# Reordering the loads of an attention and expert kernel: the first v in halves, q and k two steps ahead, the conversions of v early in a step

## The chip, the cores and the metric

The kernel runs on one core of a Trainium2 chip. The metric is device time in microseconds (us) of one launch; lower is better. A core has a matrix engine (TensorE, PE in the profile; its weight loads are PEld), three engines that work on rows of memory (VectorE or DVE, ScalarE or ACT, GpSimd or POOL), and a queue engine (SyncE, SP). Each engine works through its own list of instructions in order and waits where it needs another's result. Transfers between main memory and the core's on-chip memory (DMA) are issued here by POOL (the profile's queue q0, which can convert float32 to 16 bits on the way) and by SP (queue q1, which copies). Both queues share the same 16 DMA engines.

## What is computed

Sliding-window attention over 8 batches, 8 heads, 576 positions and 64 columns, then, for each batch, one expert of eight, chosen from the mean over the positions:

```python
mask = (rel >= 0) & (rel < 64)                       # attention, per batch and head
attn = softmax(where(mask, q @ k.T / 8, -1e9))
x    = attn @ v                                      # to [batch, 576, 512]
...
logits = x.mean(axis=1) @ w_gate                     # the gate, per batch
e      = argmax(logits);  g = softmax(logits)[e]
out    = g * (relu(x @ w1[e]) @ w2[e])               # 512 -> 1024 -> 512
```

The weights of an expert can be fetched only when the gate of its batch is known.

## The kernel before

The work of attention is cut into 16 units: unit u is one half of a batch (four heads), so batch b has the units 2b and 2b+1. A unit goes through these functions:

- `load_qk(u)` (line 208) issues two DMAs from POOL, q and k of the unit, 288 KB each on the chip, into six rotating buffers.
- `load_v(b)` (line 217) loads v of a whole batch as float32. The DMA is issued by SP, but a one-column memset on POOL in the same buffer stands ahead of it, so that it starts only when POOL has come to that place in its own list. There are two buffers.
- `transpose_qk` (line 324) turns q or k on PE; `leave_qk` (line 337) copies q out on ACT, and k on DVE unless told otherwise.
- `scores(u, c)` (line 361), c = 0 to 2: the products on PE, the exponential on ACT (line 384), the mask on DVE (line 386).
- `cast_part(u, part)` (line 300) makes the 16-bit copies of v that the products with v need: "whole" converts the unit's half of v into `va`, "low" and "high" copy it, shifted, into `vb`; `cast_v(u)` does all three. All stand on DVE unless told otherwise. The first of them is what waits for the DMA of v.
- `values(u, s)` (line 393), s = 0 and 1: the products with v on PE (line 408), then the division by the row sums on DVE (lines 422 and 424). It needs all three masked score blocks and the copies of v.
- `transpose_x(u)` (line 436) turns the result on PE, and copies it out with sums on ACT, from which DVE builds the input of the gate.

When both units of batch b are done, `gate(b)` (line 482) runs one small matmul (line 484), a maximum and its place on DVE (lines 488 and 490), and POOL loads the number of the expert into a register. Then `load_w1(b)` and `load_w2(b)` fetch 1 MB each (on the chip) through POOL. `expert_up` (line 543) is eight chunks with w1, `expert_down` (line 563) five with w2, whose results DVE copies and SP sends out.

Everything stands in an order written out by hand: `P(...)` keeps program order. Ahead of the loop the first four units are written out one call after another; `busy(n)` issues n matmuls on nothing, which keep PE at work. Then comes a loop over steps t = 4 to 19. Step t holds the scores and values of unit t, the transposes and conversions of unit t+1, and a share of the chunks of the experts, given out by `experts(pace)`. On even steps the gate of batch t/2 − 1 follows, with its loads.

In this version q and k are loaded up to four units ahead: before the loop as far as unit 6, at t = 4 unit 7 behind w2, at t = 5 the units 8 and 9, then unit t+4. The conversions of unit t+1 are spread over the second half of step t: "whole" after the transpose of q, "low" after `values(t, 0)`, "high" after `values(t, 1)`. w1 of batch 0 comes in four quarters, and `expert_up(0, ft)` uses quarter ft // 2.

## Time and profile before

| | |
|---|---|
| three runs, median (lowest to highest) | 235.81 us (235.61 to 236.13) |
| the profiled execution's own time | 237.41 us |
| its span, first to last instruction | 235.7 us |
| mean granted TensorE clock | 0.973 |
| busy: PE, PEld, DVE, ACT, POOL | 207.7, 141.4, 142.3, 121.5, 42.8 us |
| read from main memory, written | 61.90 MB, 9.44 MB |

The timeline of an engine gives start, duration, engine, line, operation, output<-input, shape and count; in brackets stands the engine's idle time ahead of it and what ended that. The chain of waits goes back from the last instruction and names at each step what had to end; its rows are start, duration, what. The DMA view of a stretch of time gives the packets and bytes of each queue, and for each kind of transfer issued there the time from issue to landing. The table of stretches gives the busy time of each engine within each stretch, with the granted TensorE clock.

### The profile page before, as it was taken

Reading aid. Unit: us, or ns where it says so; the run is one execution under the profiler, and the core shown is the slowest. Engines: PE = TensorE matmul, PEld = TensorE weight load, DVE = VectorE, ACT = ScalarE, POOL = GpSimd, SP = SyncE. Lnnn points to the kernel's source line nnn. Section 1 sums busy time; section 2 is a strip of 40 time slices with the busy share of each in tenths; the row PEclk is TensorE's granted clock in tenths of the full one; section 3 lists DMA queues with packets and bytes.
Section 4 is the critical chain, followed back from the end, with each engine's and each line's share of the span. In section 5 each row is a group of like instructions: output and inputs, shape, how many; then the busy total and the mean of one; then the engine's idle time right before and its main releaser. Section 6 shows DMA issues by size and latency. Waiting matters only on the chain.

```text
span 235.7 us, 7000 instructions
## 1 busy us (share of the span) xinstructions
PE 207.7 (88%) x3020; PEld 141.4 (60%) x3020; DVE 142.3 (60%) x315; ACT 121.5 (52%) x205; POOL 42.8 (18%) x72
## 2 busy tenths in 40 slices
PE   7657879979799978999899989999999999998980
PEld 2427557725478545875578556865687558647640
DVE  2559597539856594838764697559675964531140
ACT  2461576933376606693467617680758265605500
POOL 7252192041300160007000330020001100200000
PEclk9995899979999999999999999999999999999997
DMA  5999299999999999997999999999960995199342
GB/s 76 221 216 256 47 116 220 236 243 246 228 247 265 246 243 250 230 247 152 228 244 235 198 180 261 229 253 173 246 177 3 161 233 169 11 197 237 116 145 66
DMA packets 31222, 45.64 MB, mean 194 GB/s; under 512 B 2512, under 2 KB 22992, under 8 KB 31184
## 3 DMA queue, kind: packets, MB, share of 16 engines
q0 software_dynamic: 15152, 26.22, 63.2%
q1 hardware_dynamic: 15232, 18.88, 26.7%
q8 instruction: 25, 0.41, 0.7%
q10 hardware_dynamic: 800, 0.03, 0.2%
q14 instruction: 13, 0.11, 0.1%
HBM read 61.90 MB, written 9.44 MB: 303 GB/s over the span
## 4 chain that ended last, share of the span: by engine, by line
PE 46%; DMA 24%; ACT 11%; DVE 11%; issue 3%; POOL 1%; POOLq 1%; SPq 0%
PE php L555 23%; DMA w1t<-in_moe_w_dram 19%; PE pso L569 9%; DMA vn<-in_v_dram 5%; PE tp L329 5%; PE op L408 4%; ACT xT L453 4%; ACT pt L384 4%; ACT hT L559 3%; DVE vb L298 2%; DVE dst L298 2%; DVE pt L386 2%; PE tp L445 2%; DVE ob L572 1%; PE sp L369 1%
## 5 line engine op out<-in xcount | busy, mean ns | idle before, releaser
L555 PE MATMUL php<-xT,w1t 128*128 128x288 f16 x512 | 71.5, 288 | 5.3 <-DMA w1t<-in_moe_w_dram 4.7
L559 ACT ACTIVATE hT<-php,gatew 128x576 f16<-128x576 f32 x64 | 47.4, 746 | 33.3 <-PE php L555 33.3
L569 PE MATMUL pso<-w2t,hT 128*128 128x512 f16 x256 | 61.6, 386 | 2.6 <-DMA w2t<-in_moe_w_dram 1.8
L555 PEld LDWEIGHTS <-w1t 128*128 128x128 f16 x512 | 53.6, 113 | 13.3 <-DMA w1t<-in_moe_w_dram 5.6
L384 ACT ACTIVATE pt<-sp 128x768 f16<-128x768 f32 x48 | 37.7, 813 | 13.8 <-PE sp L369 13.8
L569 PEld LDWEIGHTS <-hT 128*128 128x128 f16 x256 | 23.4, 99 | 29.2 <-issue 3.0
L453 ACT ACTIVATE xT<-tp 128x576 f16<-128x576 f16 x28 | 17.9, 646 | 33.5 <-PE tp L445 33.5
L572 DVE COPY ob<-pso 128x512 f32<-128x512 f32 x32 | 21.9, 685 | 19.9 <-PE pso L569 19.6
L386 DVE TENSOR_TENSOR pt<-pt,masks 128x768 f16<-128x768 f16 x42 | 23.1, 557 | 17.3 <-ACT pt L384 16.8
L531 POOL DMA_DIRECT2D w1t<-in_moe_w_dram x7 | 5.0, 717 | 139.0 <-DVE gatew L513 75.1
L424 DVE TENSOR_TENSOR x<-op,linv 128x640 f16<-128x640 f32 x32 | 26.4, 824 | 1.1
L342 ACT COPY dst<-tp 128x1152 bf16<-128x1152 bf16 x16 | 18.0, 1124 | 12.1 <-PE tp L329 12.1
L298 DVE COPY dst<-tp 128x1152 bf16<-128x1152 bf16 x15 | 20.3, 1350 | 4.3 <-PE tp L329 4.0
L408 PE MATMUL op<-vb,pt 128*64 128x65 f16 x320 | 17.7, 202 | 4.1 <-DVE vb L298 3.5
L408 PEld LDWEIGHTS <-pt 128*64 128x64 f16 x640 | 14.4, 116 | 10.7 <-issue 6.0
L408 PE MATMUL op<-va,pt 128*64 128x65 f16 x320 | 17.4, 202 | 0.0
L369 PE MATMUL sp<-dst 64*64 64x128 bf16 (+1 forms) x672 | 15.4, 214 | 1.9 <-DVE dst L298 1.9
L298 DVE CAST va<-vn 128x1152 f16<-128x1152 f32 x16 | 12.7, 796 | 5.9 <-DMA vn<-in_v_dram 5.8
L298 DVE COPY vb<-va 64x1152 f16<-64x1152 f16 (+1 forms) x30 | 15.8, 527 | 0.6
L369 PEld LDWEIGHTS <-dst 64*64 64x64 bf16 x672 | 10.4, 106 | 8.9 <-issue 4.4
L476 DVE SCALAR_TENSOR_TENSOR gpart<-wg,pooled,gpart 128x8 f32<-128x8 f32 x21 | 4.8, 226 | 17.9 <-ACT xT L453 17.9
L445 PE MATMUL tp<-identh,x 128*128 128x128 f16 x160 | 11.6, 220 | 3.3 <-DVE x L424 2.5
(69 smaller groups left out, 166.6 us busy)
## 6 DMA issues: line engine op xcount, KB each, us to landing
w2t<-in_moe_w_dram POOLq DMA_DIRECT2D x8, 1024.0 KB, 17.5
out_dram<-ob SPq DMA_DIRECT2D x32, 256.0 KB, 8.6
w1t<-in_moe_w_dram POOLq DMA_DIRECT2D x7, 1024.0 KB, 10.2
qn<-in_q_dram POOLq DMA_DIRECT2D x16, 288.0 KB, 15.3
kn<-in_k_dram POOLq DMA_DIRECT2D x16, 288.0 KB, 16.5
w1t<-in_moe_w_dram POOLq DMA_DIRECT2D x4, 256.0 KB, 6.1
out_dram<-ob SPq DMA_DIRECT2D x16, 64.0 KB, 6.5
vn<-in_v_dram SPq DMA_DIRECT2D x8, 0.2 KB, 18.1
```

What stands on the lines that cost most here:

```text
L298: P(eng.tensor_copy(out=out, in_=in_))
L342: P(nc.scalar.copy(out=dst.rearrange("p (x r t) -> p x r t", x=2, t=NT), in_=view))
L369: P(nc.tensor.matmul(out=sp[64 * half:64 * half + 64, s, 64 * (qblk - 6 * c):64 * (qblk - 6 * c) + n], lhsT=kT[64 * s:64 * s + 64, ts(kblk ...
L384: P(nc.scalar.activation(out=pt, in_=sp[:, :, 0:384], func=AF.Exp, scale=scale))
L386: P(nc.vector.tensor_tensor(out=pt, in0=pt, in1=masks[:, c].rearrange("p s g w -> p s (g w)"), op=ALU.mult))
L408: P(nc.tensor.matmul(out=op[64 * half:64 * half + 64, xx, 65 * jj:65 * jj + 65], lhsT=pt[:, s, 64 * (g % 6):64 * (g % 6) + 64], rhs=win, s ...
L424: P(nc.vector.tensor_tensor(out=x[:, :, h0 * D:(h0 + 2) * D].rearrange("p j (x c) -> p x j c", x=2), in0=view[:, :, :, 0:64], in1=li[:, :, ...
L453: P(nc.scalar.activation(out=xT[:, kb, :], in_=tp[:, kl, 0:S], func=AF.Copy, accum_out=pooled[:, b, kb:kb + 1]))
L555: P(nc.tensor.matmul(out=php[:, sc, 0:288], lhsT=w1t[:, kb, cols], rhs=xT[:, kb, ts(sc, 288)], start=(kb == 0), stop=(kb == KB - 1)))
L559: P(nc.scalar.activation(out=hT[:, ft].rearrange("p (sc s) -> p sc s", sc=2), in_=php[:, :, 0:288], func=AF.Relu, scale=gatew[:, b:b + 1]))
L569: P(nc.tensor.matmul(out=pso[:, 0, :], lhsT=hT[:, fb, ts(mt, 128)], rhs=w2t[:, fb, :], start=(fb == 0), stop=(fb == FB - 1)))
L572: P(nc.vector.tensor_copy(out=ob, in_=pso[:, 0, :]))
```

## The change

- `load_v(0)` is issued as two DMAs of half the batch each, and v has three buffers.
- `load_v` can be tied to another tile: POOL then copies one column out of that tile instead of the memset. `load_v(2)` is tied so to the first part of w1 of batch 0.
- The three `scores(0, c)` stand ahead of the loads of units 2 and 3 and of v of batch 1, and the one-column copy that holds these back now reads the first score block of unit 0 instead of its k.
- `load_qk(4)` follows directly, before the first gate. After the first gate come w1, w2, unit 5 and v of batch 2; unit 6 is no longer there.
- w1 of batch 0 comes in two halves, w2 of batch 0 in the same layout as the others.
- In the loop `load_qk(t + 2)` stands behind w1 on even steps and behind v on odd ones. `load_v(3)` moves from ahead of the loop into step 4, behind the gate, w1 and unit 6.
- From t = 5 on the conversions of unit t+1 stand ahead of the mask of block 0 ("whole"), behind it ("low") and behind the mask of block 1 ("high"); step 4 converts unit 5 at its end in one go.
- "whole" of unit 1 and the copy of k of unit 3 move from DVE to ACT; some `busy` calls are shorter or stand elsewhere, and `pool_mm(0)` stands ahead of the second transpose of unit 2.

```diff
-    vpool = ctx.enter_context(tc.tile_pool(name="vpool", bufs=2))
+    vpool = ctx.enter_context(tc.tile_pool(name="vpool", bufs=3))
...
-    def load_v(b):
+    def load_v(b, behind=None):
         vn = vpool.tile([128, NM, D], FP32, tag="vn")
-        P(nc.gpsimd.memset(vn[:, 0, 0:1], 0.0))
-        P(nc.sync.dma_start(out=vn, in_=vv[b]))
+        parts = 2 if b == 0 else 1
+        for i in range(parts):
+            m = slice(i * NM // parts, (i + 1) * NM // parts)
+            if behind is None:
+                P(nc.gpsimd.memset(vn[:, m, :][:, 0, 0:1], 0.0))
+            else:
+                P(nc.gpsimd.tensor_copy(out=vn[:, m, :][:, 0, 0:1], in_=behind))
+            P(nc.sync.dma_start(out=vn[:, m, :], in_=vv[b][:, m, :]))
...
-    NQ = 4
+    NQ = 2
...
-    after = const.tile([128, 1], BF16)
-    P(nc.gpsimd.tensor_copy(out=after, in_=kt_tiles[0][:, 0:1]))
+    for c in range(3):
+        scores(0, c)
+
+    after = const.tile([128, 1], FP16)
+    P(nc.gpsimd.tensor_copy(out=after, in_=pt_tiles[0, 0][:, 0, 0:1]))
     load_qk(2)
     load_qk(3)
     load_v(1)
-    for c in range(3):
-        scores(0, c)
+    load_qk(4)
...
-    cast_part(1, "whole")
...
+    cast_part(1, "whole", A)
...
     gate(0, False)
     load_w1(0)
-    cast_v(2)
-    load_qk(4)
-    load_v(2)
     load_w2(0)
     load_qk(5)
-    load_qk(6)
+    load_v(2, w1_parts()[:, 0, 0, 0:1])
+    cast_v(2)
...
-    transpose_qk(3, 1)
+    transpose_qk(3, 1, leave=False)
+    leave_qk(3, 1, A)
     cast_v(3)
-    busy(4)
+    busy(3)
...
     transpose_x(3)
-    load_v(3)
...
             gate(b)
             load_w1(b)
-            if START + 1 < t < NU - 4:
-                load_qk(t + 4)
+            if t + 2 < NU:
+                load_qk(t + 2)
+            if t == START + 1:
+                load_v(3)
             load_w2(b)
-            if t == START + 1:
-                load_qk(7)
...
-        for u in [8, 9] if t == 5 else [t + 4] if t % 2 == 1 else []:
-            if u < NU:
-                load_qk(u)
+        if t % 2 == 1 and t + 2 < NU:
+            load_qk(t + 2)
         if prev:
             transpose_x(t - 1)
+        if ahead and t > START + 1:
+            cast_part(t + 1, "whole")
...
+        if ahead and t > START + 1:
+            cast_part(t + 1, "low")
         if on:
             scores(t, 1)
+        if ahead and t > START + 1:
+            cast_part(t + 1, "high")
...
-            cast_part(t + 1, "whole")
...
-            cast_part(t + 1, "low")
...
-            cast_part(t + 1, "high")
...
+        if t == START + 1:
+            cast_v(5)
```

More of the change, by code (lines that the diff above doesn't have):

```diff
@@ L544, in expert_up @@
         if b == 0:
-            w1t, cols = w1_parts()[:, ft // 2], slice(ft % 2, 256, 2)
+            w1t, cols = w1_parts()[:, ft // 4], slice(ft % 4, 512, 4)
         else:
@@ L697 @@
         scores(1, c)
-    busy(2)
+    cast_part(1, "whole", A)
+    busy(1)
     values(0, 0)
@@ L792 @@
             values(t, 0)
-        if ahead:
-            cast_part(t + 1, "low")
         experts(pace)
```

15 lines of the change are left out of this document (6 added, 9 removed).

## The prediction

> **What bounds the kernel now.** The page first: which engine has the work, and which the chain of waits names.
>
> ```profile
> PE 207.7 (88%) x3020; PEld 141.4 (60%) x3020; DVE 142.3 (60%) x315; ACT 121.5 (52%) x205; POOL 42.8 (18%) x72
> DMA  5999299999999999997999999999960995199342
> PE 46%; DMA 24%; ACT 11%; DVE 11%; issue 3%; POOL 1%; POOLq 1%; SPq 0%
> ```
>
> PE works for 207.7 of 235.7 us, so what remains to win or lose is waiting in PE's own list. The 16 DMA engines are full over three quarters of the span, so a transfer's place in its queue decides when it lands. PE's timeline around the first gate of the loop (gl at 47.00; I call this time g) shows the two largest waits behind the start:
>
> ```profile
> 47.00 0.39 PE L484 MATMUL gl<-gpart,onesf 128*128 128x8 f32 x2 [0.42 <-DVE gpart L476]
> 49.45 3.31 PE L569 MATMUL pso<-w2t,hT 128*128 128x512 f16 x8 [1.77 <-DMA w2t<-in_moe_w_dram]
> 52.99 1.90 PE L569 MATMUL pso<-w2t,hT 128*128 128x512 f16 x8
> 64.78 1.17 PE L555 MATMUL php<-xT,w1t 128*128 128x288 f16 x8 [1.68 <-DMA w1t<-in_moe_w_dram]
> ```
>
> w2 of batch 0 costs 1.77 us, w1 of batch 1 1.68 us. The eight matmuls behind the first wait take 3.31 instead of 1.90 us; the table of stretches tells why:
>
> ```profile
> 49.00:52.30 3.30, 2.85 (x7) 1.04 (x8) 0.16 (x1) 0.69 (x1) 2.35 (x4) 0.50 1.17 242
> ```
>
> The granted clock (the 0.50) was half there: 1.4 us more. How the queues share the engines is read from the DMA view of 62 to 67, 52 to 55, 109 to 113 and 34 to 38 us, in this order:
>
> ```profile
> q0 software_dynamic: 232, 0.89, 87.7%
> q1 hardware_dynamic: 233, 0.24, 17.2%
> ```
>
> ```profile
> q0 software_dynamic: 348, 0.37, 72.2%
> q1 hardware_dynamic: 353, 0.36, 42.7%
> ```
>
> ```profile
> q0 software_dynamic: 148, 0.61, 102.0%
> ```
>
> ```profile
> q0 software_dynamic: 1193, 0.67, 123.1%
> ...
> vn<-in_v_dram SPq DMA_DIRECT2D x1, 0.2 KB, 18.5
> ```
>
> With both queues filled, each gets as many packets as the other, whatever their size: 46 per us beside weights (1 MB in 256 packets of 4 KB), 117 beside q and k (288 KB in 256 packets). Weights alone run at 37 per us. In the fourth stretch q1 has no row, though a v is under way (18.5 us from issue to landing; DVE takes it up at 52.4, so it was issued at about 33.9): a v takes over 4 us to its first packet. A v is 1152 packets of 1 KB.
>
> **The change part by part.**
>
> *Start to g.* DVE's timeline has the first conversion, and the chain of waits what follows:
>
> ```profile
> 15.86 0.76 DVE L298 CAST va<-vn 128x1152 f16<-128x1152 f32 x1 [1.54 <-DMA vn<-in_v_dram]
> ```
>
> ```profile
> 27.52 0.68 DVE va L298
> 30.74 0.73 DVE xT L298 x2
> 33.50 2.07 PE php L555 x16
> 69.07 0.44 PE op L408 x20
> ```
>
> ```profile
> vn<-in_v_dram SPq DMA_DIRECT2D x1, 0.2 KB, 13.3
> ```
>
> The halved v lets the conversions begin at 15.86 − 1.54 = 14.3, clear of POOL's beside them, and gate 0 may come up to 3 us sooner. But that gain meets v of batch 1, issued at 13.66, landed (last row) at 26.96. Now POOL holds it, units 2 and 3 back until the first score block, 1.3 us later, and unit 4's 512 packets follow beside it: q1 stays at 117 per us until about 26, and v lands near 29. From its conversion to the last xT takes 31.47 − 27.52 = 3.95 us of DVE's list: xT at 33.0, php at 33.1 instead of 33.50. I take −0.3; bounds −2.4 (v as before, php then at w1's landing, about 31.1) and +1.0 (PE idles there and loses clock). The copy of k moved to ACT, `busy` and w1 in halves lie beside this wait: nothing; without that cover they are inside these bounds.
>
> *w2 of batch 0, w1 of batch 1.* With units 4 and 6 out of their way both land in time: 1.77 + 1.4 + 1.68 = 4.9 us won by t = 5. The Trainium skill ("TensorE: Matmul & The Clock Gate", What's actually happening) has PE return to half clock after an idle window of about 3.4 us; the trace halves it after 2.2 us of waits, so by the skill the wait's end would win 1.4 us less.
>
> *v of batch 3, the term that decides.* `load_v(3)` moved from 38 us to behind gate 1, w1(1) and unit 6 in POOL's list.
>
> ```profile
> 49.95 0.71 POOL L531 DMA_DIRECT2D w1t<-in_moe_w_dram  x1 [11.88 <-DVE gatew L513]
> ```
>
> w1 is issued at g + 2.95; three more issues of 0.72 put v(3) at g + 5.3 and its first packet at g + 9.5. w1 flows from about g + 4.4 and has moved 190 of 256 packets by then; the rest gives v 66 by g + 10.9, unit 6 512 more by g + 15.3, w2(1) 256 by g + 20.8, and unit 7 the last 318 by g + 23.5; about 1 us to landing: g + 24.5. Before, it landed at about 69 us, g + 22:
>
> ```profile
> 69.05 0.76 DVE L298 CAST va<-vn 128x1152 f16<-128x1152 f32 x1 [1.03 <-DMA vn<-in_v_dram]
> 105.12 0.56 DVE L386 TENSOR_TENSOR pt<-pt,masks 128x768 f16<-128x768 f16 x1 [0.77 <-ACT pt L384]
> 105.59 0.17 DVE L488 MAX8 gmx<-gl 128x8 f32<-128x8 f32 x1
> ```
>
> There it stood behind the masks of unit 5 and held back 1.03 us of DVE alone. Now "whole" of unit 6 is ahead of them: DVE's list stops at it, and PE's at `values(5, 0)`, which the 4.9 us won bring forward to about g + 17. After landing DVE needs 0.76, three masks of 0.56 and two shifted copies of about 0.46: 3.35 us. `values(5, 0)` ends at g + 28.0 instead of 69.51 = g + 22.5: +5.5, the 4.9 swallowed within it. Bounds: +2 if v starts at once after its issue, +7 if one more MB-long turn of slow packets falls on it. The Trainium skill ("DMA: Bandwidth & Descriptors", Latency and other measured facts) gives about 600 ns to a first byte of such a queue; by it v lands 3.6 us sooner and this term is near +2; the silent stretch at 34 to 38 us speaks for the longer one.
>
> *Clock.* PE idles some 9 us there. Restarted, it should run at half clock as at 49 us; PE waits for DVE in part of it: +1.0 (0 to 2.5).
>
> *Two steps ahead.* Unit t+2 now lands just behind w1 where unit t+4 did. The landings of the DMAs issued at 107.58 and 108.29 (t = 8) and at 134.20 (t = 10), then the chain:
>
> ```profile
> w1t<-in_moe_w_dram POOLq DMA_DIRECT2D x1, 1024.0 KB, 10.6
> qn<-in_q_dram POOLq DMA_DIRECT2D x1, 288.0 KB, 12.7
> ```
>
> ```profile
> qn<-in_q_dram POOLq DMA_DIRECT2D x1, 288.0 KB, 11.8
> ```
>
> ```profile
> 107.58 10.61 DMA w1t<-in_moe_w_dram
> ...
> 119.41 0.62 PE tp L329 x18
> ...
> 144.04 0.62 PE tp L329 x18
> ...
> 204.34 8.72 DMA w1t<-in_moe_w_dram
> ```
>
> That slot landed at 120.98 and 146.0. In the new kernel it holds units 10 and 12, which PE turns at 119.41 and 144.04: 1.6 and 2.0 us of new wait. Against it a less filled queue may bring w1 sooner (10.6 us at t = 8): −1.1 and −0.4. For t = 12, whose slot was empty, I take +1.35, an estimate below both. By the same comparison the loads of odd steps, and k, have 0 to 3 us to spare.
>
> *Conversions early in a step.* A shifted copy on DVE, and PE's longest wait for DVE:
>
> ```profile
> 110.15 0.44 DVE L298 COPY vb<-va 64x1152 f16<-64x1152 f16 x1
> ```
>
> ```profile
> 87.96 0.73 PE L445 MATMUL tp<-identh,x 128*128 128x128 f16 x10 [1.51 <-DVE x L424]
> ```
>
> On even steps two of about 0.46 and one of 0.75 come ahead of the gate's maximum. Two fit before the mask of block 1 (DVE waited 0.77 for it), the last goes between 105.12 and 105.59: w1, issued behind it, is 0.46 later. What it frees late in a step (that 1.51 and smaller ones) turns into wait for w1 or q, except at batch 2, whose w1 also has a free queue: −0.6 there. Sum for batches 3 to 5: (0.46 − 1.1 + 1.6) + (0.46 − 0.4 + 2.0) + 1.35 = 4.4; bounds 1 and 8.
>
> *Sum.* −0.3 + 5.5 + 1.0 − 0.6 + 4.4 = +10.0. On the profiled execution (span 235.7, its time 237.41 with 1.7 around) this is 247.4; its time is 1.6 over the median of 235.81, so about 245.8 for unprofiled runs. I say 245.5.
>
> **The rivals.**
> - *v(3) comes in time* (q1 served first, or an earlier gate): no stall and no lost clock, 4.9 won. 235.8 − 0.3 − 4.9 − 0.6 + 4.4 = 234.4, and 230 if the short prefetch costs nothing. Against it: equal packet counts, and an issue that no gate lets happen sooner.
> - *The stall stays, the steps run free*: w1 lands 2 us sooner at every gate, and q behind it just in time. 235.8 − 0.3 + 5.5 + 1.0 − 0.6 = 241.4. For it: w1(7), with little beside it, took 8.72 us.
> - *Every step waits*: k as well as q, and v(3) with its upper bounds: 235.8 + 1 + 7 + 2.5 − 0.6 + 6 = 251.7.
> - *The loads move nothing*: DMA is full either way, landings differ by less than their cover: 235.8.
>
> **How the numbers follow.** Forecast (243 to 249) 0.47; free steps 0.21; every step 0.17; v in time 0.12; nothing 0.03. The range 238 to 251.5 holds the first two and much of the third. About 0.2% (0.5 us) can be told from no change. Slower 0.85, same 0.03, faster 0.12.
>
> **What would show it.** DVE idle for 8 to 11 us ahead of va in step 5, ended by v; PE idle as long at line 408 (415 in the new listing); half clock behind it; no wait at w2 of batch 0 or w1 of batch 1; PE's transposes of units 10, 12 and 14 waiting for q. It is wrong if v(3) lands before g + 17, or if q of unit t+2 is there when PE asks for it.

## The result

| | before | after |
|---|---|---|
| median of the runs side by side (lowest to highest) | 235.97 us (235.61 to 236.30, 4 runs) | 256.35 us (254.70 to 257.66, 4 runs) |
| ratio to before, 95% interval | | 1.0861 [1.0793, 1.0928] |
| the profiled execution's own time, its span | 237.41, 235.7 us | 254.70, 253.0 us |
| mean granted TensorE clock | 0.973 | 0.958 |

The change makes the kernel 20.4 us slower. The forecast was 245.5 us, with a range that ended at 251.5, and the time lies outside it: the direction was right, but the loss forecast (9.7 us) is half of the one that came.

First the page of the changed kernel: the work of the engines, the DMA row of the 40 slices, the queues, and the chain of waits by engine and by line.

```profile
PE 210.6 (83%) x3014; PEld 143.0 (57%) x3014; DVE 138.8 (55%) x313; ACT 123.7 (49%) x207; POOL 40.8 (16%) x71
...
DMA  6999999269999029996999979995999399079431
...
q0 software_dynamic: 13840, 26.22, 58.7%
q1 hardware_dynamic: 18704, 18.88, 25.6%
...
DMA 38%; PE 36%; ACT 9%; DVE 8%; POOL 3%; issue 3%; POOLq 0%; SPq 0%; DVEq 0%
PE php L560 19%; DMA qn<-in_q_dram 19%; DMA vn<-in_v_dram 13%; PE pso L574 7%; PE tp L336 4%; DMA w1t<-in_moe_w_dram 3%; ACT xT L460 3%; PE op L415 3%; ACT pt L391 3%; ACT hT L564 2%; DMA kn<-in_k_dram 2%; DVE pt L393 2%; POOL w1t L537 1%; PE tp L452 1%; DVE dst L305 1%
```

PE's work grew by 2.9 us only, the span by 17.3: the rest is waiting. In the chain, DMA went from 24% to 38%. Two kinds of transfer carry it now, q (19%) and v (13%, 5% before), while w1 fell from 19% to 3%. (The chain counts a transfer from its issue to its landing; what PE waited for it is less.) The DMA row shows gaps: a slice of 6.3 us is at 2 ahead of 50 us, and two are at 0 and 2 around 88, where the row of before has, in its first 175 us, one 2 only, at its start. There the 16 engines stand still until a gate has come up, and then everything is wanted at once. The gaps go with the late v(3), not with the shorter distance of q and k: in the runs below, e3 (v(3) late, q and k far ahead) has a 3 and a 0 at these two places, and e1 (v(3) early, q and k close) nothing under 7. The chain in order of time names the links:

```profile
15.50 13.67 DMA vn<-in_v_dram
33.72 3.76 PE php L560 x16
...
53.92 19.97 DMA vn<-in_v_dram
...
93.06 12.41 DMA qn<-in_q_dram
...
119.49 11.66 DMA qn<-in_q_dram
...
146.39 11.76 DMA qn<-in_q_dram
...
173.40 11.96 DMA qn<-in_q_dram
```

Start and duration: v(1) from 15.50, v(3) from 53.92 to 73.89, then q of the units 8, 10, 12 and 14, each some 12 us from its issue to its landing; PE's waits for these four q add up to 6.7 us. The timelines of PE and of DVE show what waits for them. The start, PE:

```profile
23.91 0.39 PE L490 MATMUL gl<-gpart,onesf 128*128 128x8 f32 x2 [0.28 <-DVE gpart L673]
...
30.33 0.54 PE L376 MATMUL sp<-dst 64*64 64x64 bf16 x28 [1.24 <-ACT dst L303]
33.36 0.36 PE L376 MATMUL sp<-dst 64*64 64x64 bf16 x14 [2.50 <-DVE xT L305]
33.65 3.82 PE L560 MATMUL php<-xT,w1t 128*128 128x288 f16 x16
...
48.98 0.39 PE L490 MATMUL gl<-gpart,onesf 128*128 128x8 f32 x2 [0.40 <-DVE gpart L482]
49.59 1.90 PE L574 MATMUL pso<-w2t,hT 128*128 128x512 f16 x8
...
62.87 1.14 PE L560 MATMUL php<-xT,w1t 128*128 128x288 f16 x8 [0.24 <-DVE ob L577]
```

Gate 0 comes 2.5 us sooner than before (26.39), and gate 1 2.0 later: between them PE waits 1.24 and 2.50 us for copies, and its first 16 matmuls with w1 take 3.76 us in the chain, where they took 2.07, at half clock (the table at the end of this section). Behind gate 1 the waits for w2(0) (1.77) and w1(1) (1.68) are gone, as forecast. DVE in front of the same place, and in front of the stall in step 5:

```profile
29.26 0.76 DVE L305 CAST va<-vn 128x1152 f16<-128x1152 f32 x1 [4.21 <-DMA vn<-in_v_dram]
...
73.98 0.76 DVE L305 CAST va<-vn 128x1152 f16<-128x1152 f32 x1 [10.56 <-DMA vn<-in_v_dram]
74.65 0.55 DVE L393 TENSOR_TENSOR pt<-pt,masks 128x768 f16<-128x768 f16 x1
```

PE behind that, up to the next gate, and the first and the longest of its waits for q:

```profile
75.26 0.26 PE L415 MATMUL op<-vb,pt 128*64 128x65 f16 x1 [8.12 <-DVE pt L393]
76.09 0.26 PE L415 MATMUL op<-vb,pt 128*64 128x65 f16 x1 [0.45 <-DVE pt L393]
77.17 0.26 PE L415 MATMUL op<-vb,pt 128*64 128x65 f16 x1 [0.65 <-DVE pt L393]
...
88.73 0.28 PE L490 MATMUL gl<-gpart,onesf 128*128 128x8 f32 x2
...
105.51 0.69 PE L336 MATMUL tp<-ident,qn 128*64 128x128 bf16 x18 [1.40 <-DMA qn<-in_q_dram]
...
158.20 0.69 PE L336 MATMUL tp<-ident,qn 128*64 128x128 bf16 x18 [2.13 <-DMA qn<-in_q_dram]
```

The mask that PE waits for stands directly behind the conversion in DVE's list: DVE isn't short of time, it stands still for 10.56 us. The waits for q(10) and q(14) are 1.42 and 1.75. The table of stretches (length, busy time of each engine, granted clock, DMA share, GB/s) for the two places of half clock:

```profile
33.90:37.30 3.40, 3.40 (x16) 1.99 (x14) 2.48 (x6) 1.49 (x2) 0.00 (x0) 0.50 1.06 217
71.40:81.70 10.30, 5.33 (x51) 3.46 (x52) 5.04 (x9) 0.74 (x1) 0.00 (x0) 0.50 1.09 275
```

### The profile page after: what moved, and what is told of

Read it like the earlier page. It is cut to its first block, busy times and chain, and to the rows that moved or that the text cites. A ratio compares the mean times of both kernels' runs of the same rounds, so it can differ in the third digit from the quotient of the medians.

```text
span 253.0 us, 6980 instructions
## 1 busy us (share of the span) xinstructions
PE 210.6 (83%) x3014; PEld 143.0 (57%) x3014; DVE 138.8 (55%) x313; ACT 123.7 (49%) x207; POOL 40.8 (16%) x71
## 2 busy tenths in 40 slices
DMA packets 33382, 45.64 MB, mean 180 GB/s; under 512 B 7104, under 2 KB 25408, under 8 KB 33344
## 3 DMA queue, kind: packets, MB, share of 16 engines
q1 hardware_dynamic: 18704, 18.88, 25.6%
## 4 chain that ended last, share of the span: by engine, by line
DMA 38%; PE 36%; ACT 9%; DVE 8%; POOL 3%; issue 3%; POOLq 0%; SPq 0%; DVEq 0%
PE php L560 19%; DMA qn<-in_q_dram 19%; DMA vn<-in_v_dram 13%; PE pso L574 7%; PE tp L336 4%; DMA w1t<-in_moe_w_dram 3%; ACT xT L460 3%; PE op L415 3%; ACT pt L391 3%; ACT hT L564 2%; DMA kn<-in_k_dram 2%; DVE pt L393 2%; POOL w1t L537 1%; PE tp L452 1%; DVE dst L305 1%
## 5 line engine op out<-in xcount | busy, mean ns | idle before, releaser
L560 PE MATMUL php<-xT,w1t 128*128 128x288 f16 x512 | 74.6, 296 | 3.2 <-DMA w1t<-in_moe_w_dram 1.9
L560 PEld LDWEIGHTS <-w1t 128*128 128x128 f16 x512 | 55.5, 116 | 12.1 <-DMA w1t<-in_moe_w_dram 2.5
L574 PE MATMUL pso<-w2t,hT 128*128 128x512 f16 x256 | 60.2, 380 | 1.9 <-DVE ob L577 0.8
L391 ACT ACTIVATE pt<-sp 128x768 f16<-128x768 f32 x48 | 37.8, 813 | 11.1 <-PE sp L376 11.1
L415 PE MATMUL op<-vb,pt 128*64 128x65 f16 x320 | 17.3, 198 | 12.1 <-DVE pt L393 11.2
L415 PEld LDWEIGHTS <-pt 128*64 128x64 f16 x640 | 13.8, 112 | 19.2 <-DVE pt L393 12.3
L305 DVE COPY dst<-tp 128x1152 bf16<-128x1152 bf16 x14 | 19.0, 1356 | 9.2 <-PE tp L336 9.1
L376 PE MATMUL sp<-dst 64*64 64x128 bf16 (+1 forms) x672 | 16.1, 217 | 5.3 <-DVE xT L305 2.5
L305 DVE CAST va<-vn 128x1152 f16<-128x1152 f32 x15 | 11.6, 770 | 14.8 <-DMA vn<-in_v_dram 14.8
L376 PEld LDWEIGHTS <-dst 64*64 64x64 bf16 x672 | 10.9, 108 | 12.8 <-issue 7.9
L336 PE MATMUL tp<-ident,qn 128*64 128x128 bf16 x288 | 11.1, 221 | 7.1 <-DMA qn<-in_q_dram 6.7
L305 DVE COPY vb<-va 64x1152 f16<-64x1152 f16 (+1 forms) x30 | 14.9, 496 | 0.5
## 6 DMA issues: line engine op xcount, KB each, us to landing
qn<-in_q_dram POOLq DMA_DIRECT2D x16, 288.0 KB, 11.9
```

The costliest lines, as they stand in the source:

```text
L305: P(eng.tensor_copy(out=out, in_=in_))
L336: P(nc.tensor.transpose(out=tp[64 * s:64 * s + 64, ts(t, 128)], in_=src[:, s, ts(t, D)], identity=ident, tile_position=(0, 64 * s)))
L376: P(nc.tensor.matmul(out=sp[64 * half:64 * half + 64, s, 64 * (qblk - 6 * c):64 * (qblk - 6 * c) + n], lhsT=kT[64 * s:64 * s + 64, ts(kblk ...
L391: P(nc.scalar.activation(out=pt, in_=sp[:, :, 0:384], func=AF.Exp, scale=scale))
L415: P(nc.tensor.matmul(out=op[64 * half:64 * half + 64, xx, 65 * jj:65 * jj + 65], lhsT=pt[:, s, 64 * (g % 6):64 * (g % 6) + 64], rhs=win, s ...
L560: P(nc.tensor.matmul(out=php[:, sc, 0:288], lhsT=w1t[:, kb, cols], rhs=xT[:, kb, ts(sc, 288)], start=(kb == 0), stop=(kb == KB - 1)))
```

## The experiments

The labels e, c and b stand for an edit of the changed kernel, a kernel of its parts, and an edit of the kernel before. The theory after this reading has three costs: v(3), which lands late and holds DVE's list; q, which lands late in every even step; and the start. One part of the change, the early conversions, shows only waits under 1 us of its own in the trace. All ratios are to the kernel before, run on the same chip beside the experiment; a ratio isn't the quotient of the two medians, and differs from it by up to 0.8% (e4). The table gives the start of a gate's matmul, and the end, in each profiled execution (us), from their traces:

| | gate 1 | gate 2 | gate 5 | gate 7 | end |
|---|---|---|---|---|---|
| before | 47.00 | 78.78 | 154.75 | 201.47 | 235.68 |
| after | 48.98 | 88.73 | 168.97 | 218.43 | 252.98 |
| e1 | 47.54 | 75.38 | 156.11 | 205.50 | 240.20 |
| e2 | 49.04 | 84.87 | 164.55 | 212.86 | 247.42 |
| e3 | 49.90 | 89.89 | 165.42 | 213.05 | 247.50 |
| c1 | 49.19 | 77.01 | 152.76 | 200.39 | 234.52 |
| c2 | 48.32 | 75.39 | 149.77 | 196.50 | 230.99 |
| b1 | 47.09 | 82.27 | 155.95 | 202.69 | 237.29 |
| b3 | 46.76 | 76.65 | 154.83 | 203.20 | 237.81 |
| b4 | 47.58 | 84.23 | 160.63 | 208.29 | 243.18 |
| e5 | 47.31 | 86.35 | 166.28 | 215.56 | 252.89 |
| c5 | 46.05 | 74.04 | 148.46 | 195.19 | 230.85 |

### Undoing one part of the change

**e1: v(3) back ahead of the loop.**

```diff
     transpose_x(3)
+    load_v(3)
...
-            if t == START + 1:
-                load_v(3)
```

> The changed kernel with one thing undone: load_v(3) stands again behind transpose_x(3), ahead of the step loop, instead of in the group of gate 1. Theory (v(3) lands at 73.9 us and the conversion va of v(3) holds VectorE's order from 63.4 to 74.0, so that values(5,0) wait 8.1 us on TensorE, and the clock is halved behind it): v(3) lands before 60, no wait over 1 us at values(5,0), the first gate matmul of batch 2 at 77 to 79.5 us instead of 88.7, all later marks earlier by the same 9 to 12 us, the waits for q(8), q(10), q(12), q(14) stay (1.4 to 2.1 us each): 243 to 246 us. Rival 1 (the conversions moved up in a step are what stalls the step, whichever v they wait for): no more than 3 us gained, 252 us or more. Rival 2 (v(3) back in its place delays w1(1), q and k of the first gate's batches, which gives the gain back): the gate of batch 2 at 82 or later, 247 to 251.

Measured: 244.57 us, ratio 1.0359 [1.0302, 1.0415], so 11.8 us less than the changed kernel. v(3) landed at 52.4, values(5, 0) waited no longer, and gate 2 came at 75.38, 13.4 us sooner (77 to 79.5 had been expected). Not all of that is v(3)'s: gate 1 came 1.4 us sooner too, though PE and DVE have the same lists ahead of it as in the changed kernel. PE waited for xT here as well (2.68 us), but the 16 matmuls behind it ran at full clock (2.15 us). From gate 1 to gate 2 the gain is 11.9 us. The waits for q stayed (1.30, 1.59, 2.27, 1.69; the second ended together with a mask of DVE, and the profile names that). Both rivals fall.

**e2: the conversions back in their old places, v(3) still late.**

```diff
-        if ahead and t > START + 1:
-            cast_part(t + 1, "whole")
...
             transpose_qk(t + 1, 0)
+            cast_part(t + 1, "whole")
...
             values(t, 0)
+        if ahead:
+            cast_part(t + 1, "low")
```

("high" goes behind `values(t, 1)` in the same way, and the block conversion of unit 5 is gone.)

> The changed kernel with the conversions of v in the places of the kernel before (whole behind the first transposes of the next unit, low behind values(t,0), high behind values(t,1), nothing for unit 5 as a block), v(3) still late. Theory (the landing of v(3) is the cause, and an early place only lets more work queue behind the waiting conversion): v(3) lands at about 74 all the same, the wait on TensorE gets shorter but stays, since unit 5's values need the conversion: the first gate matmul of batch 2 at 83 to 87 instead of 88.7, and the end 2 to 6 us earlier: 249 to 253. Rival 1 (the place of the conversion is the whole of the loss): the wait is gone, 246 or less. Rival 2 (the early places are worth something in steps 6 to 15, which this takes away again): the distance from the gate of batch 2 to the end grows by over 1 us, 253 to 257.

Measured: 247.62 us, ratio 1.0444 [1.0401, 1.0487]; that is 8.7 us less, more than was expected, with gate 2 at 84.87 as expected. DVE and PE of this run:

```profile
74.07 0.76 DVE L305 CAST va<-vn 128x1152 f16<-128x1152 f32 x1 [7.96 <-DMA vn<-in_v_dram]
```

```profile
75.87 0.26 PE L415 MATMUL op<-vb,pt 128*64 128x65 f16 x1 [6.20 <-DVE x L431]
```

The conversion starts as late as without the edit, but the masks of unit 5 are now ahead of it, and PE waits only 6.20 us, for a division behind it. So the place of the conversion decides how much hangs on a late v.

**e3: q and k four steps ahead again, v(3) still late.**

```diff
     load_v(2, w1_parts()[:, 0, 0, 0:1])
+    load_qk(6)
...
-            if t + 2 < NU:
-                load_qk(t + 2)
+            if START + 1 < t < NU - 4:
+                load_qk(t + 4)
...
             load_w2(b)
+            if t == START + 1:
+                load_qk(7)
...
-        if t % 2 == 1 and t + 2 < NU:
-            load_qk(t + 2)
+        for u in [8, 9] if t == 5 else [t + 4] if t % 2 == 1 else []:
+            if u < NU:
+                load_qk(u)
```

> The changed kernel with the loads of q and k in the step loop as in the kernel before (unit 6 ahead of the loop, unit 7 behind w2 in step 4, 8 and 9 in step 5, then four steps ahead); v(3) still in the group of gate 1. Theory (two steps ahead, q lands 1.4 to 2.1 us after TensorE is ready for it in each of the steps 7, 9, 11 and 13): the four waits of together 6.7 us vanish, the distance from the first gate matmul of batch 2 to the end falls from 164.3 to 157 to 159 us, v(3) lands at about 71 (q and k of unit 6 no longer ahead of it), so the wait at values(5,0) falls from 8.1 to about 5: 244 to 250 us. Rival (the waits are only moved: with q there, TensorE waits in the same steps for w1, which then shares the queues with more of q and k): the distance from the gate of batch 2 to the end stays over 162, and 251 or more.

Measured: 249.27 us, ratio 1.0512 [1.0462, 1.0562], 7.1 us less. All four waits for q are gone, and gate 2 to the end takes 157.6 instead of 164.3 us. But the wait at values(5, 0) stayed at 8.11 us, where 5 had been expected: v(3) landed at 74.5 although unit 6 no longer stood ahead of it, with w2(1) and the units 7 to 9 issued right behind v in the other queue. The forecast's own count of packets would have said so: 66 of v beside the rest of w1(1), 256 beside w2(1) and the other 830 beside q and k at 117 per us end at about g + 23.6, and 1 us to landing makes g + 24.6, an estimate. It landed at that, 24.6 us behind this run's gate 1.

**c1: both loads undone (the edits of e1 and e3 together).**

> Both of the edits above that move loads: v(3) ahead of the loop, and q and k four steps ahead as in the kernel before. What stays of the change is its start (v(0) in two halves, unit 4 and w1 and w2 of batch 0 in the new order) and the conversions early in a step. Theory (the late v(3) and the short distance of q and k are all of the loss behind gate 1; the start costs about 2 us): the end at 234 to 237 us, a time of 236 to 239, and a ratio of 1.000 to 1.013 to the kernel before. Rival 1 (the early conversions are worth something once nothing late stands behind them): below 235. Rival 2 (the early conversions cost by themselves): 240 or more, with waits of TensorE for VectorE at values in the steps 6 to 15.

Measured: 236.78 us, ratio 1.0015 [0.9994, 1.0036]: the two moved loads, undone together, give back all of the 20 us within the noise. What is left, the start and the early conversions, comes out at nothing. That can be two nothings or two effects that cancel; the next run tells.

**c2: c1 with the conversions in their old places too (the edit of e2). Only the start of the change is left.**

> The kernel with v(3) ahead of the loop and q and k four steps ahead (c1), and in addition the conversions of v in the step loop in the places of the kernel before. What stays of the change is its start alone. Theory (the early conversions cost or win nothing by themselves once no v is late; they only let more stand behind a v that is late): within 1 us of c1, 235.8 to 237.8. Rival 1 (they win something in each step): 238 or more. Rival 2 (they cost, through masks and the gate's maximum that stand behind them on even steps): 235.5 or less, and then faster than the kernel before, since the first gate matmul of batch 2 stands 1.8 us earlier in c1 than there.

Measured: 233.33 us, ratio 0.9855 [0.9783, 0.9927]. The theory that the conversions cost nothing by themselves falls, and rival 2 holds: they cost some 3.5 us, and the start, with w2(0) and w1(1) in time, wins 3.1. The two traces are 3.5 us apart as well, but 0.9 of it lies ahead of gate 1 (49.19 against 48.32), where both kernels have the same code, so 2.7 can be the conversions'. Two waits of PE in c1 that are far shorter in c2 show where a part of it sits:

```profile
79.01 1.24 PE L574 MATMUL pso<-w2t,hT 128*128 128x512 f16 x5 [0.79 <-DVE ob L577]
...
106.74 0.22 PE L415 MATMUL op<-vb,pt 128*64 128x65 f16 x1 [0.78 <-DVE pt L393]
```

and in c2, at the same two places:

```profile
76.79 1.89 PE L574 MATMUL pso<-w2t,hT 128*128 128x512 f16 x8 [0.20 <-DVE ob L577]
...
104.35 0.22 PE L415 MATMUL op<-vb,pt 128*64 128x65 f16 x1 [0.17 <-DVE pt L393]
```

The copies stand ahead of the masks and of the copies of w2's results in DVE's list, and PE needs both.

### One part alone, added to the kernel before

**b1: v(3) behind w1(1) alone.**

```diff
     transpose_x(3)
-    load_v(3)
...
             load_w1(b)
+            if t == START + 1:
+                load_v(3)
```

> The kernel before with one part of the change alone: load_v(3) behind w1(1) in the group of gate 1. The price of this part among the others was 11.8 us (two steps ahead) and 12.5 us (four steps ahead). Theory (what v(3) costs is its landing, some 21 us behind its issue, less the work that stands ahead of its conversion in VectorE's list): issued at about 51 us it lands at 71 to 73 instead of 69; the conversion stands behind the masks of unit 5 here, so that values(5,0) run and only x and what follows wait, 2 to 4 us, and w1(1), with no v beside it, wins back up to 1.7: 236.5 to 241. Rival 1 (the price belongs to the place of the load, whatever stands around it): 246 or more. Rival 2 (v(3) lands as before, since it waited for v(2) and for slow packets anyway): 235.8 or less.

Measured: 239.61 us, ratio 1.0163 [1.0094, 1.0231]: 3.8 us, a third of what the same move costs inside the change. DVE and PE:

```profile
72.64 0.76 DVE L298 CAST va<-vn 128x1152 f16<-128x1152 f32 x1 [6.00 <-DMA vn<-in_v_dram]
```

```profile
74.44 0.26 PE L408 MATMUL op<-vb,pt 128*64 128x65 f16 x1 [4.24 <-DVE x L424]
```

v(3) lands 1.3 us sooner than inside the change (72.6 against 73.9), and the conversion stands behind unit 5's masks: PE stalls 4.24 instead of 8.12 us.

**b2 and b4: the early conversions alone,** the same kernel measured twice.

```diff
+        if ahead and t > START + 1:
+            cast_part(t + 1, "whole")
...
-            cast_part(t + 1, "whole")
```

("low" and "high" as in the change; unit 5 in one go at the end of step 4.)

> The kernel before with the early conversions alone (whole ahead of the first score block, low and high around the second, unit 5 as a block behind step 4). In the changed kernel with all loads in time they made 236.8 of 233.3 us against different runs of before, a ratio of 1.0015 instead of 0.9855, that is 3.8 us. Theory (the copies stand ahead of the masks and of the gate's maximum on even steps and ahead of x of the step before; each batch loses 0.4 to 0.8 us): 237.5 to 240.5. Rival (that difference came from the start or from the chip, the conversions by themselves cost nothing): 235.5 to 237.

Four times between 239.89 and 244.66 us, too far apart for an interval. The second measurement:

> Once more the kernel before with the early conversions alone, whose four times lay between 239.9 and 244.7, too far apart for an interval. Theory (the conversion of unit 6 now stands ahead of the masks of unit 5, so that TensorE waits for v(3) at values(5,0) even where v(3) is loaded as before and lands at 67.7, and may lose clock behind it; and each later gate is 0.4 to 0.5 later): all times above 238.5, gate 2 3 to 5 us later than before, 239 to 245. Rival (the first look was a disturbed one): 235.5 to 238.

Measured: 241.24 us, ratio 1.0147 [1.0102, 1.0192], 3.5 us by the ratio. Its trace is of its longest execution (244.82 us), so its sizes need not hold for the others; there DVE stands at the conversion of unit 6, with v(3) loaded where it always was:

```profile
69.93 0.76 DVE L298 CAST va<-vn 128x1152 f16<-128x1152 f32 x1 [3.75 <-DMA vn<-in_v_dram]
```

So this v had never been early. Before the change the wait for it, 1.03 us, lay behind everything that PE needed; the early place alone makes it a stall, of DVE for 3.75 us and of PE, at `values(5, 0)`, for 1.30.

**b3: q and k two steps ahead alone.**

```diff
     load_qk(5)
-    load_qk(6)
...
-            if START + 1 < t < NU - 4:
-                load_qk(t + 4)
+            if t + 2 < NU:
+                load_qk(t + 2)
```

(Unit 7 behind w2 and the list for odd steps go as in the change.)

> The kernel before with q and k two steps ahead alone. Theory (the loads' short distance costs by itself, whatever else the change does: unit 6 lands about 12 us behind gate 1, the units 8, 10, 12 and 14 each 1.4 to 2.1 us after TensorE is ready for them; it was 7.1 us beside a late v(3) and 7.8 us beside one in time): waits for q in the steps 7 to 13, 1.2 to 2.3 us each, none at w2(0) or w1(1) beside unit 6, 241 to 244. Rival 1 (the waits arise only with the early conversions, which bring TensorE to the transposes sooner): 239 or less. Rival 2 (the mis-sized term of the prediction was right here: 4.4 us less 0 to 2 won at w1): 238 to 240.9.

Measured: 240.99 us, ratio 1.0203 [1.0156, 1.0250], between the ranges of the theory and of rival 2. Gate 2 comes 2.1 us sooner (no wait for w1(1); that for w2(0) stayed, 1.89, which had not been expected), and 4.3 are lost from there to the end: waits of 1.16, 2.35 and 1.57 us for q(10), q(12) and q(14), and none for q(8), which landed at 91.12, just ahead of its transposes at 91.40.

**e4: two steps ahead, but q and k ahead of w1** (on e1).

```diff
             load_w1(b)
-            if t + 2 < NU:
-                load_qk(t + 2)
...
+            if t + 2 < NU:
+                load_qk(t + 2)
             load_w1(b)
```

> The kernel with v(3) ahead of the loop and q and k still two steps ahead (the first of the experiments), with one edit: in the even steps q and k of unit t+2 are loaded ahead of w1 instead of behind it. Theory (two steps ahead leaves no room: w1 and q of an even step are wanted within 4 us of each other, and w1 has no slack, 1.2 us of wait at batch 2 already): the waits for q(8), q(10), q(12), q(14) go, but w1 of the batches 2 to 6 lands 3 to 5 us later, and TensorE waits as much for it in each: 250 to 262. Rival 1 (the order alone was at fault; w1 is later only by the two issues of 1.4 us and the waits for q were as long): 242 to 247. Rival 2 (nothing is late any more): 240 or less.

Measured: 257.79 us, ratio 1.0822 [1.0716, 1.0929]. In the trace (of its longest execution, 258.75 us) the waits for q are gone, and w1 is late instead:

```profile
98.64 1.63 PE L560 MATMUL php<-xT,w1t 128*128 128x288 f16 x6 [5.42 <-DMA w1t<-in_moe_w_dram]
...
130.31 1.35 PE L560 MATMUL php<-xT,w1t 128*128 128x288 f16 x8 [3.66 <-DMA w1t<-in_moe_w_dram]
```

Neither of the two orders behind the gate is good. Loading q and k in the time ahead of it, as four steps ahead did, leaves neither wait (c1: none for q, 1.25 us for w1(2)); an order in between, q ahead of w1 and k behind it, was not run.

### The start

**c3: unit 4 behind w1(0)** (on c1: `load_qk(4)` moves from behind `load_v(1)` to behind `load_w1(0)`).

> c1 with one thing more undone: load_qk(4) stands behind w1(0) instead of ahead of gate 0. Theory (beside unit 4's 512 packets v(1) lands at 29.4 us instead of 27.0; VectorE's list stands 4.2 us ahead of its conversion, TensorE 2.4 us ahead of the copies behind it, and then starts its first w1 matmuls at half clock): v(1) lands at 26 to 27.5, no half clock between 33 and 38 us, the first 16 w1 matmuls take 2.1 instead of 3.7 us, the first gate matmul of batch 1 at 46 to 47.5 instead of 49.2, and a time of 234 to 235.5. Rival 1 (TensorE then waits for w1(0), which lands at 32.3 and 34.8, and loses the clock all the same): v(1) earlier, but the gate of batch 1 at 48.5 or later and 236 to 237.5. Rival 2 (unit 4, now behind w1(0), is late for its transposes at 44.5): a wait for q(4) or k(4) of over 1 us, 237 or more.

Measured: 239.95 us (235.42 to 241.95), ratio 1.0148 [1.0065, 1.0230]. In the profile, of the fastest execution, v(1) came at 27.20 instead of 29.54 and gate 1 at 47.30, as expected; but the half clock stayed (16 matmuls in 3.53 us), and the other executions were 4 to 6.5 us longer. What they lost it on isn't in that profile, and the ratio rests mostly on them; this one stays open.

**c4: the conversion of unit 2 behind the transposes of unit 3** (on c1).

```diff
-    cast_v(2)
...
     leave_qk(3, 1, A)
+    cast_v(2)
     cast_v(3)
```

> c1 with cast_v(2) moved behind the transposes of unit 3, so that the masks of unit 2, the copies xT and the copy of k stand ahead of it in VectorE's list; every load stays as in c1. Theory (it is the place of the waiting conversion that stops TensorE, and v(1)'s landing at 29.4 is early enough for values(2,0)): VectorE waits for v(1) later and for under 2 us, TensorE's wait for xT of 2.4 us ahead of unit 3's scores goes, no half clock between 33 and 38 us, the gate of batch 1 at 46 to 47.5 instead of 49.2, 234 to 235.5. Rival 1 (TensorE waits for w1(0) instead, the clock still halves): gate of batch 1 at 48.5 or later, 236 to 237.5. Rival 2 (values(2,0) then wait for the conversion): a wait of TensorE of over 1 us at values(2,0), 236.5 or more.

Measured: 236.27 us, ratio 0.9962 [0.9915, 1.0009]. The wait for xT went, and gate 1 came at 47.48, but the wait for w1(0) took over, with the half clock behind it:

```profile
32.21 3.73 PE L560 MATMUL php<-xT,w1t 128*128 128x288 f16 x16 [2.52 <-DMA w1t<-in_moe_w_dram]
```

That is rival 1's mechanism, with part of the theory's gain.

**c6: v(0) in one piece** (on c2: `parts = 1`).

> The kernel that keeps only the start of the change (c2, 233.3 us), with v(0) loaded in one piece again. Theory (the halves have packets of 256 B instead of 1 KB and still bring the first conversion 1.5 to 2 us forward, and with it the gate of batch 0; the rest of the start, w1 and w2 ahead of the v, is what wins): v(0) lands at about 16 to 17 us, the gate of batch 0 at 23.5 to 25 instead of 22.3, most of it lost again in VectorE's wait for v(1): 233 to 235. Rival 1 (the halves are the win): 236 or more. Rival 2 (the small packets slow unit 1 and cost): under 232.8.

Measured: 233.35 us, ratio 0.9879 [0.9817, 0.9940]: no different from c2. Gate 0 is at 25.00 instead of 22.30, and the 2.7 us that the halves win there are lost again in the wait for v(1). The halves are worth nothing here.

**c5 and c7: c2 with c4's edit and twelve idle matmuls,** measured twice.

```diff
     for c in range(3):
         scores(3, c)
+    busy(12)
```

> The start of the change alone (c2) with two edits: cast_v(2) behind the transposes of unit 3, and twelve idle matmuls on spin ahead of the first w1 matmuls. Theory (TensorE waits 3.8 us for VectorE in c2 and then runs w1(0) at half clock for 3.4 us): the wait for xT goes, TensorE is kept busy until w1(0) lands at about 32, the first 16 w1 matmuls take 2.1 to 2.5 instead of 3.7 us, the gate of batch 1 at 45.5 to 47 instead of 48.3, 231 to 233. Rival (w1(0), then v(1)'s conversion, set the time whatever TensorE does in the wait): the gate of batch 1 at 47.5 or later, 233 to 234.5.

Measured: 232.58 us, ratio 0.9865 [0.9798, 0.9933], gate 1 at 46.05. PE:

```profile
29.82 2.76 PE L647 MATMUL idle<-spin 128*128 128x512 bf16 x12
32.42 2.12 PE L560 MATMUL php<-xT,w1t 128*128 128x288 f16 x16
```

The same wait for w1(0), but filled with work on nothing: the clock stays up, and the 16 matmuls take 2.12 instead of 3.73 us. Once more:

> Once more the start of the change with cast_v(2) behind the transposes of unit 3 and twelve idle matmuls (c5), on another chip job, to see whether it stays ahead of the kernel before: 231.5 to 234, a ratio of 0.98 to 0.992. If the gain was that chip's: within 0.5% of the kernel before.

Measured: 233.05 us, ratio 0.9804 [0.9766, 0.9843]. This version is faster than both kernels; that it beats c2 is not shown (the intervals overlap). The trace of c7 is of a longer execution (235.75 us): there half clock lay from 25.10 to 31.93, ahead of the idle matmuls, and gate 1 came at 48.79, but the 16 matmuls behind them took 2.12 us here too.

**e5: the same two edits in the changed kernel.**

```diff
-    cast_v(2)
...
+    cast_v(2)
     cast_v(3)
...
+    busy(12)
```

> The changed kernel with two edits at its start: cast_v(2) behind the transposes of unit 3, and twelve idle matmuls ahead of the first w1 matmuls; nothing else is undone. Theory (the start's loss, 2 us at gate 1 where a gain of 0.3 was forecast, comes from VectorE standing ahead of v(1) and the half clock behind it, and all behind gate 1 hangs on gate 1, v(3) too, so that it passes through whole): no half clock between 33 and 38 us, gate 1 at 46 to 47, v(3) landing 24 to 25 us behind it, gate 2 at 85.5 to 87, and a time 2 to 3 us under the changed kernel's: 253 to 254.5. Rival (v(3)'s landing is set by the DMA engines' load and not by gate 1, so that the stall swallows what the start wins): gate 2 at 88 or later, 255.5 to 257.

Measured: 256.23 us, ratio 1.0851 [1.0776, 1.0926], the time of the changed kernel. The marks went as the theory had it: gate 1 1.7 us sooner, v(3) 24.7 us behind it (72.05, the start of the conversion, against 73.98), gate 2 2.4 and gate 7 2.9 us sooner. At the very end of this profile the gain is lost:

```profile
228.29 9.70 PE L560 MATMUL php<-xT,w1t 128*128 128x288 f16 x64 [2.13 <-DMA w1t<-in_moe_w_dram]
```

The wait for w1(7) is 2.13 us where it was 0.97, and the clock is halved behind it (64 matmuls in 9.70 instead of 8.03 us). Why w1(7) landed later behind its gate than in the changed kernel is open. So in this trace the start's gain passes through the stall at v(3), but does not reach the end.

## Why the prediction was right in direction and wrong in size

The time came out 10.9 us above the forecast. The term that decides, v(3), was right. Three steps failed: the early conversions were priced at 0.3 us and cost 3.5, two steps ahead at 3.5 and cost 7.1, and the start was to win 0.3 us, with at most 1.0 of lost clock, where gate 1 came 2.0 later and the clock alone cost 1.7.

The runs let the 20 us be added up along one line, from the kernel before to the changed one, one part at a time. The forecast's terms are put beside each step:

| from, to | part | forecast | measured |
|---|---|---|---|
| before, c2 | start, w2(0) and w1(1) in time | −0.3 − 4.9 = −5.2 | −3.1 (236.43 to 233.33) |
| c2, c1 | early conversions | −0.6 + 2 · 0.46 = +0.3 | +3.5 (233.33 to 236.78) |
| c1, e3 | v(3) late, with its clock | 5.5 + 4.9 + 1.0 = +11.4 | +12.5 (236.78 to 249.27) |
| e3, after | two steps ahead | 4.4 − 0.9 = +3.5 | +7.1 (249.27 to 256.35) |
| | sum | +10.0 | +20.0 |

(The 4.9 stands in two rows because the forecast let the stall swallow it; the two 0.46 were counted within its 4.4. The runs of before beside these kernels had medians from 235.8 to 236.8, so a row is good to about 1 us; the sum of the parts is 0.4 short of the 20.4 measured side by side.)

- *v(3), the term that decides:* right, in mechanism and nearly in size. The forecast had it land at g + 24.5; it landed at 73.89 = g + 24.9. DVE stood still for 10.56 us at the place named, PE for 8.12 behind it. The first matmul with w1(1) came 1.9 us sooner than before (62.87), and `values(5, 0)` ended 8.1 later (77.60 in the chain): 10.0 us lost between them, where 5.5 + 4.9 = 10.4 had been forecast. The packets came as counted: the first of q1 behind its issue shows at 58.2 to 58.4, g + 9.3 (forecast g + 9.5). e1 against the changed kernel and e3 against c1 price it at 11.8 and 12.5.
- *w2(0) and w1(1) in time:* right. Gate 1 to the first matmul with w1(1) took 13.89 instead of 17.78 us: 3.9 of the 4.9.
- *Start to g:* wrong, by 2.3 us and outside its bounds. The landing of v(1) was forecast near 29 and came at 29.2. php was put at 33.1 and began at 33.7, near it. What failed is the term for the clock behind that wait: PE had waited 1.24 and 2.50 us of the last five, and ran its first 16 matmuls at half clock. The forecast had named that danger and given it 1.0 us as its bound; it cost 1.7 (3.76 against 2.07). c4 and c5 show it: the same wait for w1(0), without and with idle matmuls, 3.73 and 2.12 us. The wait alone doesn't decide it: e1, with the same lists of PE and DVE there and 2.68 us of wait, ran them in 2.15 us, and its gate 1 came at 47.54.
- *Clock behind the stall:* +1.0 forecast; half clock lasted 10.2 us, with PE at work for 5.3 of them. Gate 2 was 9.95 us late where `values(5, 0)` had been 8.1 late, so about 1.9; within its bounds.
- *Conversions early in a step:* failed. The forecast priced the 0.46 us that stand ahead of the gate's maximum, and credited 0.6 at batch 2 for what they free. It put at nothing that masks and the copies of w2's results stand behind the same conversions (c1 beside c2), and, in the kernel before, that any v that isn't early turns into a stall (b4). They cost 3.5 us by the medians. Nor did the credit come: the wait for x that they shorten in batch 2 (1.50 us in c2, 0.47 in c1) turns into a longer wait for w1(2) (0.66 and 1.25). They also have a part in the 12.5 us that the late v(3) costs inside the change, against 3.8 alone (b1): e2, with the conversions back and v(3) late, wins 8.7 us, some 5 more than their own 3.5. They are not the whole difference, for with the conversions in the same place PE stalls 6.20 us in e2 and 4.24 in b1. The forecast had their part in the stall, as a part of v(3).
- *Two steps ahead:* the mechanism was right, q of each even step landing 1.4 to 2.1 us late; the size failed. By the gates of the profile (conversions counted in), batch 3 (gate 3 to 4) lost 1.0 us and batch 4 2.4, where 0.96 and 2.06 had been forecast. It failed at the two ends. Batch 2 had been given a free queue and a gain of 0.6; it waited 1.40 for q(8) and lost 0.9. Batch 5 lost 2.2 instead of 1.35, and 0.9 more came behind gate 6. Alone, in the kernel before, the same distance costs 4.2 us (b3), not far from the forecast's 3.5. What comes on top inside the change lies in part at batch 2: q(8) is late in the changed kernel and in e1 (1.40 and 1.30 us), which have the early conversions, and in time in b3 and e2, which don't. The rest of it is open.
- *The base:* the two traces differ by 17.3 us, the medians by 20.4, since the trace of before is of an execution 1.4 us over its median and that of the changed kernel of its fastest, 1.65 under it. So what was read from gates above leaves out some 3 us. The longer executions of the changed kernel had a lower granted clock (0.951 to 0.954 against 0.958); in which stretches is not known.

Of the rivals, "v(3) comes in time" is what e1 made by hand: the forecast had 11.1 us between it and the likeliest case, the run 11.8. "The stall stays, the steps run free" is e3: 4.1 forecast, 7.1 measured. The range ended at 251.5, just short of "every step waits" at 251.7. No case had the conversions cost several us by themselves, and the two ends of two steps ahead beside it.

## What to carry to other kernels

A transfer that nothing waits for is early only as long as its consumer stands behind the other work of that engine: before moving the consumer forward in an in-order list, look when its data lands, not whether there was a wait before. Loads behind a gate share one burst of bandwidth, so what doesn't depend on the gate belongs ahead of it: behind it, either q or w1 came late. And where PE must wait anyway for some 2 us, matmuls on nothing can keep the clock up (16 matmuls in 2.12 instead of 3.73 us), though here no gain of the whole kernel was shown for them alone.

## What the runs showed of the hardware

*The clock is decided by windows, not by the length of one wait.* In the traces the stretches at half clock, but for the one that the end cuts off, last 3.41 us or a multiple (3.41, 6.83, 10.24, and 13.65 in e3), and in one trace they start whole multiples of it apart (in the changed kernel at 33.86 and 71.41, eleven windows). Which wait leads to one depends on how it lies. The table of stretches for two neighbouring windows of e2, with a wait of 1.95 us for q(12) in the first of them:

```profile
149.48:152.89 3.41, 1.47 (x35) 0.85 (x33) 2.55 (x5) 0.81 (x1) 0.00 (x0) 1.00 1.17 262
152.89:156.30 3.41, 3.41 (x35) 2.09 (x32) 0.49 (x2) 1.86 (x2) 0.00 (x0) 0.50 1.08 233
```

and of e1, where the longer wait for the same q, 2.27 us, falls across the border of two:

```profile
140.93:144.34 3.41, 2.14 (x26) 0.87 (x22) 3.37 (x8) 2.05 (x3) 0.00 (x0) 1.00 1.12 267
144.34:147.76 3.42, 2.42 (x48) 2.00 (x49) 0.88 (x3) 1.63 (x2) 0.00 (x0) 1.00 1.16 249
```

PE was busy for 1.47 of 3.41 us in the first case, and the next window ran at 0.50; with 2.14 and 2.42 it stayed at full clock. But PE's busy time isn't the whole rule. Two windows of e1's start, each with the one behind it:

```profile
21.47:24.88 3.41, 2.14 (x59) 1.45 (x58) 1.78 (x8) 2.09 (x5) 0.00 (x0) 1.00 1.16 246
24.88:28.29 3.41, 3.41 (x46) 3.21 (x46) 0.00 (x0) 2.62 (x6) 2.90 (x5) 0.50 1.15 256
```

```profile
31.71:35.13 3.42, 1.54 (x24) 1.39 (x24) 3.37 (x9) 1.50 (x3) 0.25 (x2) 1.00 1.17 216
35.13:38.54 3.41, 3.41 (x61) 2.74 (x59) 2.93 (x8) 2.18 (x3) 0.00 (x0) 1.00 1.05 221
```

With 2.14 us of work the clock was halved here, with 1.54 it was not. Over all the traces, with the windows of each counted from its own half clock, every window with less than 1.5 us of work was followed by half clock. Of the windows at full clock with 1.5 to 2.7 us of work some were and some were not, and what decides there is open. (In the kernel before, the half clock that the prediction puts behind 2.2 us of waits began at 48.94, within the second of these waits, behind a window with 1.74 us of work.) The Trainium skill ("TensorE: Matmul & The Clock Gate", What's actually happening) has a free-running window of 3413 ns, which the traces agree with; the prediction read its idle window as one without any work, and these rows show that some 1.5 us of work don't save it. It also says that the transition point varies from run to run with the phase of that window; by that the same wait would cost 1.7 us in one execution and nothing in the next. The start of e1 beside that of the changed kernel, the same lists of PE and DVE with 2.15 and 3.76 us for the 16 matmuls, fits that. It would fit the spread of 3 us among the four runs of the changed kernel too, but no run here shows it as its cause.

*The halves of v(0) travel in smaller packets.* q1 of the changed kernel moved 18704 packets where it had 15232 for the same bytes, and the page counts 7104 packets under 512 B instead of 2512. c6, with v(0) whole, has 15232 again. Cutting 1152 packets of 1 KB in four each would give 3456 more, which is all but 16 of the 3472. In time it made no difference (c6 beside c2).

*SP's issues stand behind a v.* The three stores that SP issues behind v(3) took 14.35 us of its list together, and v(3) itself took 9.45 us to issue in the kernel before, behind v(2):

```profile
53.92 0.70 SPq L228 DMA_DIRECT2D vn<-in_v_dram  x1
54.67 14.35 SPq L578 DMA_DIRECT2D out_dram<-ob  x3
```

No run here tried whether that delays anything that PE needs.
